# One attention-and-MLP kernel, five written-out instruction lists settled anew

## The chip, the cores and the metric

The kernel runs on one core of a Trainium2 chip. A core has five engines that matter here, each with its own in-order list of instructions: PE (TensorE, matrix products), DVE (VectorE), ACT (ScalarE), POOL (GpSimd) and SP (SyncE, which here only starts transfers). They meet through semaphores. The metric is the device time of one execution in microseconds, the median of a few runs. Before the change it is 328.6 us, the median of three runs between 327.31 and 330.21.

## What is computed

The input x has 2048 rows of 512 numbers. Four blocks follow one another, linear attention (A) and an MLP (B), each twice with the same weights, each with a residual sum and a layer norm in front:

```python
    x = x + _A_ref(_layernorm(x, axis=-1), A_wqkv, A_wo)
    x = x + _B_ref(_layernorm(x, axis=-1), B_w1, B_b1, B_w2, B_b2)
    x = x + _A_ref(_layernorm(x, axis=-1), A_wqkv, A_wo)
    x = x + _B_ref(_layernorm(x, axis=-1), B_w1, B_b1, B_w2, B_b2)
```

Attention has 32 heads of 16 numbers. With phi(t) = (t+1 if t > 0, else exp(t)) + 1e-6 it needs the sum over all rows of phi(k) times v (`kv`) and of phi(k) (`z`), and then gives each row phi(q)·kv / (phi(q)·z), times `wo`. So no output row of an attention block can start before all rows have passed through k. The MLP normalises its input again, multiplies by `w1` (512 to 1792), applies a tanh gelu with bias, multiplies by `w2` (1792 to 512) and adds `b2`; its rows do not depend on each other.

## The kernel before, in words

The 2048 rows are 16 row tiles of 128 (numbered st, 0 to 15) in 4 chunks of 512. Every piece of work is an operation with a name, built by `Graph.op`: `K1_9` is the k product of layer 1, row tile 9. The names that are used below, with the lines that issue them:

| names | what they do, engine | line |
|---|---|---|
| statsX, aggrX, vepsX, powX, nmrX, normX | layer norm of a row tile: DVE, DVE, POOL, POOL, POOL (only when ACT normalises), DVE or ACT | 734, 736, 739 or 747, 749, 766, 774 or 769 |
| TA, TB, TP | a transposing transfer, started by SP (PTA, PTB with tcA, tcB: the same by PE and a copy) | 784, 1069 (797, 807) |
| K, Q and expk, relu, min, phi | k and q products (PE), then phi on ACT, ACT, DVE, and DVE or POOL | 852, 870 or 883; 822, 833, 826 or 835, 828 or 839 |
| G, Z, KV, M | the products that make z and kv·wo (PE), with evictions ga, gt, kvm, cpm on DVE or ACT | 953 or 985, 934, 1008, 1031 |
| D or pz, red, den, rec, pr | the denominators, by PE and ACT or by DVE and POOL | 1077 to 1085, 1053 to 1065 |
| WO, then RA | attention output (PE) and residual sum (DVE) | 1101, 1106 |
| W1, gelu | MLP up (PE), gelu (ACT) | 1133, 1139 |
| W2 (two halves, _0 and _7), RB, OD | MLP down (PE), residual sum (DVE), output transfer (SP) | 1171, 1177 or 1181, 1183 |

`W10_1_3_0` is thus `W1`, layer 0, chunk 1, column tile 3 (of 14), part 0. Chunk 0 of each layer is cut into two halves of 256 rows (parts 0 and 1); all other `W1` operations take 512 rows.

The order of the work is written out by hand as data: `CONF["ORDER"]` holds one list of names per engine, 388 names for PE, 506 for DVE, 323 for ACT, 220 for POOL, 104 for SP. Each engine plays its list in that order and nothing is reordered on the chip. While the kernel is built, `Scheduler.run` walks the five lists with a model of durations (the numbers in the `G.op` calls). The model no longer decides any order. It decides which free slot of a buffer pool or which PSUM bank each tile takes (the one that the model says is free first), and so which earlier user an operation has to wait for. `assign_waits` then turns dependences and slot reuse into semaphore waits.

PSUM has 8 banks, shared by classes: `W1` results have banks 0 to 3, `W2` and `WO` results banks 3 to 5, two at a time. Two output buffers (`NOUT`), 12 large tiles (`t4`), 10 normalised tiles (`yb`) and 8 phi(k) tiles (`pkb`) are the pools that most tiles go through. ACT holds one function table at a time; a change between exp and gelu issues a table load (line 1304).

Of the kernel before, what the change touches and what calls it, by code (L numbers as in the profile page):

```python
# [7 lines left out]
ACT = mybir.ActivationFunctionType  # L8
# [102 lines left out]
class Scheduler:  # L111
# [12 lines left out]
    def run(self):  # L124
# [14 lines left out]
        for _ in g.ops:  # L139
# [29 lines left out]
            if o.fast and pool_busy > at:  # L169
                dur += pool_busy - at - 60.0  # L170
            if o.fast:
                dve_busy = at + dur
            if e == "pool" and o.sem is None and o.dur > 300.0:
                dur += max(0.0, min(dve_busy - at, 400.0))
                pool_busy = at + dur
# [92 lines left out]
def assign_waits(graph, order, sems, dma_sems):  # L268
# [10 lines left out]
    while len(done) < total:  # L279
        moved = False  # L280
        for e in ENGINES:
# [44 lines left out]
    LAND={'x0': 3210, 'x1': 3930, 'wk1': 5300, 'wk0': 6430, 'x2': 6950, 'wq': 8450, 'xc0': 9730, 'xc1': 11020, 'xc2': 12240},  # L326
# [1041 lines left out]
```

## Time and profile before

| quantity | value |
|---|---|
| median of three runs (lowest, highest) | 328.6 us (327.31, 330.21) |
| span of the profiled execution, first to last instruction | 326.2 us |
| the profiled execution's own device time | not listed apart from its span; the median is 2.4 us above it |
| PE matmul busy | 320.6 us, 98% |
| DVE, ACT, POOL busy | 218.7 us (67%), 197.5 us (61%), 131.2 us (40%) |
| bytes moved by DMA | 20.39 MB, mean 62 GB/s |
| chain that ended last, by engine | PE 91%, DVE 4%, DMA 2%, ACT 1% |

The profile lists, per engine and line of the kernel, how long instructions ran and what the engine waited for before them. Matmuls are pipelined: one of 512 columns is listed with 379 ns, while the next one starts 216 ns after it. The time between starts is what counts for PE.

### The profile page before, as it was taken

How to read it: one execution, taken by the hardware profiler on the slowest of the kernel's cores; microseconds unless marked ns; L12 is line 12 of the kernel's file. 1: busy time of each engine (PE TensorE's matmuls, PEld its weight loads, DVE VectorE, ACT ScalarE, POOL GpSimd, SP SyncE). 2: the span in 40 equal slices, each digit the busy share in tenths (PEclk: the TensorE clock that was granted, in tenths of full speed). 3: DMA queues.
4: the chain of work that ended last, by engine and by line, in shares of the span. 5: the costliest groups of instructions: out<-in, count | busy, mean ns of one | idle time of the engine just before them, and what ended most of it. 6: DMA issues, size and time to landing. Idle time of an engine off the chain costs nothing.

```text
span 326.2 us, 4796 instructions
## 1 busy us (share of the span) xinstructions
PE 320.6 (98%) x1724; PEld 158.2 (48%) x1724; DVE 218.7 (67%) x506; ACT 197.5 (61%) x338; POOL 131.2 (40%) x224
## 2 busy tenths in 40 slices
PE   7999999999999999999999999999999999999996
PEld 3444545656544444444444444458644444444453
DVE  4998689989866662535468899999988663300132
ACT  5998889744753387357963395969923553645200
POOL 3465637673238106134139525645811275100000
PEclk9999999999999999999999999999999999999999
DMA  7424662524012400312110200111153233300011
GB/s 239 163 51 92 173 223 62 181 49 81 21 31 48 97 1 2 74 22 55 27 32 19 47 17 0 28 39 36 32 92 72 48 45 69 81 0 2 32 64 50
DMA packets 47028, 20.39 MB, mean 62 GB/s; under 512 B 41948, under 2 KB 45532, under 8 KB 47004
## 3 DMA queue, kind: packets, MB, share of 16 engines
q1 hardware_dynamic: 45676, 15.09, 20.4%
q0 software_dynamic: 1056, 4.72, 4.5%
q10 hardware_dynamic: 272, 0.26, 0.3%
q8 instruction: 14, 0.23, 0.3%
q14 instruction: 10, 0.08, 0.1%
HBM read 8.00 MB, written 2.10 MB: 31 GB/s over the span
## 4 chain that ended last, share of the span: by engine, by line
PE 91%; DVE 4%; DMA 2%; ACT 1%; SPq 1%; issue 1%; ACTq 0%
PE ps L1133 29%; PE ps L1171 26%; PE ps L1101 9%; PE ps L852 9%; PE ps L870 5%; PE ps L953 4%; PE ps L883 3%; PE ps L985 2%; DMA t<-in_A_x_dram 1%; PE ps L1158 1%; DMA t<-yb 1%; DVE t L839 1%; PE ps L1008 1%; PE ps L1077 1%; PE ps L797 1%
## 5 line engine op out<-in xcount | busy, mean ns | idle before, releaser
L1139 ACT ACTIVATE gT<-ps,b1c 128x512 bf16<-128x512 f32 (+1 forms) x140 | 76.9, 601 | 61.2 <-PE ps L1133 60.8
L1133 PE MATMUL ps<-t,w 128*128 128x512 bf16 (+1 forms) x560 | 102.2, 336 | 0.5 <-DMA t<-yb 0.3
L1171 PE MATMUL ps<-w,gT 128*128 128x512 bf16 x434 | 97.3, 379 | 0.0
L1133 PEld LDWEIGHTS ps<-t,w 128*128 128x128 bf16 x560 | 54.4, 98 | 44.5 <-DMA t<-yb 0.7
L1171 PEld LDWEIGHTS ps<-w,gT 128*128 128x128 bf16 x434 | 42.4, 98 | 50.4 <-ACT gT L1139 0.3
L822 ACT ACTIVATE eb<-ps 128x512 bf16<-128x512 f32 x56 | 32.1, 606 | 21.3 <-PE ps L852 20.3
L749 POOL TENSOR_TENSOR rstd<-veps,neghalf 128x1 f32<-128x1 f32 x64 | 36.7, 581 | 8.2 <-DVE veps L747 5.5
L1181 DVE TENSOR_TENSOR outb<-ps,xsb 128x512 bf16<-128x512 f32 x15 | 10.3, 689 | 40.3 <-PE ps L1171 32.1
L734 DVE BATCH_NORM_STATS2 stats<-xsb 128x6 f32<-128x512 f32 x48 | 32.0, 681 | 0.2
L1101 PE MATMUL ps<-gtb,t 128*128 128x512 bf16 x128 | 31.8, 379 | 0.1
L852 PE MATMUL ps<-wqkv,t 128*128 128x512 bf16 x128 | 31.1, 379 | 0.0
L769 ACT ACTIVATE yb<-xsb,nmr,rstd 128x512 bf16<-128x512 f32 x21 | 16.8, 811 | 12.6 <-POOL nmr L766 12.5
L833 ACT ACTIVATE rb<-ps 128x512 bf16<-128x512 f32 x38 | 22.3, 611 | 1.6 <-PE ps L852 0.9
L739 POOL TENSOR_SCALAR veps<-mv 128x1 f32<-128x1 f32 x32 | 7.3, 227 | 38.4 <-DVE mv L736 36.6
L774 DVE TENSOR_SCALAR yb<-xsb,mv,rstd 128x512 bf16<-128x512 f32 x27 | 15.0, 572 | 9.0 <-POOL rstd L749 8.9
L835 DVE TENSOR_SCALAR eb<-eb 128x512 bf16<-128x512 bf16 x46 | 13.6, 306 | 10.9 <-ACT eb L822 10.8
L1118 POOL TENSOR_TENSOR xsb<-xsb,b2b 128x512 f32<-128x512 f32 x14 | 17.0, 1218 | 8.1 <-DVE yb L774 6.5
L870 PE MATMUL ps<-wqkv,t 128*128 128x512 bf16 x80 | 20.2, 379 | 0.0
L747 POOL TENSOR_SCALAR veps<-mv 128x1 f32<-128x1 f32 x28 | 8.4, 305 | 28.0 <-DVE mv L736 26.9
L1101 PEld LDWEIGHTS ps<-gtb,t 128*128 128x128 bf16 x128 | 12.3, 98 | 14.9 <-ACT gtb L966 0.7
L852 PEld LDWEIGHTS ps<-wqkv,t 128*128 128x128 bf16 x128 | 12.0, 97 | 14.7 <-ACT t L807 0.9
L1065 POOL TENSOR_TENSOR t<-t,rr 128x512 bf16<-128x512 bf16 x7 | 7.7, 1100 | 24.4 <-DVE rr L1061 14.1
(103 smaller groups left out, 398.7 us busy)
## 6 DMA issues: line engine op xcount, KB each, us to landing
w<-in_B_w_dram POOLq DMA_DIRECT2D x4, 896.0 KB, 5.9
out_dram<-outb SPq DMA_DIRECT2D x15, 128.0 KB, 2.1
t<-in_A_x_dram SPq DMA_DIRECT2D x3, 512.0 KB, 7.3
t<-yb SPq DMA_TRANSPOSE x56, 2.5
wqkv<-in_A_wqkv_dram SPq DMA_DIRECT2D x1, 512.0 KB, 5.7
wo<-in_A_wo_dram POOLq DMA_DIRECT2D x1, 512.0 KB, 6.6
wqkv<-in_A_wqkv_dram POOLq DMA_DIRECT2D x1, 512.0 KB, 4.5
t<-t SPq DMA_TRANSPOSE x20, 2.5
```

The lines of the kernel that those rows point to most:

```text
L734: G.op("dve", lambda e: e.bn_stats(stats[:, s.slot, :], src()), 620, reads=src_keys, writes=[k + "s"], tiles=[s, *src_tiles], prio=prio, n ...
L749: G.op("pool", lambda e: e.tensor_tensor(rstd[:, s.slot:s.slot + 1], veps[:, s.slot:s.slot + 1], neghalf[:], op=ALU.pow), 570, reads=[k + ...
L769: G.op("act", lambda e: e.activation(yb[:, y.slot, :], src(), ACT.Identity, bias=nmr[:, s.slot:s.slot + 1], scale=rstd[:, s.slot:s.slot + 1]),
L822: G.op("act", lambda e: e.activation(eb[:, et.slot, :], bank(bt), ACT.Exp, scale=factor()), 478, reads=[src_key, *more], writes=[f"e{tag}" ...
L833: G.op("act", lambda e: e.activation(rb[:, rt.slot, :], bank(bt), ACT.Relu, scale=factor()), 478, reads=[src_key, *more], writes=[f"r{tag} ...
L852: ins = e.matmul(bank(b), lhsT=yTa(yT)[:, dt, k * P:(k + 1) * P], rhs=wqkv[:, dt, D:2 * D], start=(dt == 0), stop=(dt == DT - 1))
L870: ins = e.matmul(bank(b), lhsT=yTa(yT)[:, dt, k * P:(k + 1) * P], rhs=wqkv[:, dt, 0:D], start=(dt == 0), stop=(dt == DT - 1))
L1101: ins = e.matmul(bank(wb), lhsT=yTa(pq)[:, kt, k * P:(k + 1) * P], rhs=gtb[:, kt, :], start=(kt == 0), stop=(kt == DT - 1))
L1118: G.op("pool" if on_pool else "dve", lambda e: e.tensor_tensor(xsb[:, st, :], xsb[:, st, :], b2b[:], op=ALU.add), 1120 if on_pool else 600 ...
L1133: ins = e.matmul(bank(b, n), lhsT=w1[:, dt, ft * P:(ft + 1) * P], rhs=yTa(yT)[:, dt, k0 * P:k1 * P], start=(dt == 0), stop=(dt == DT - 1))
L1139: G.op("act", lambda e, ft=ft, b=b, k0=k0, k1=k1, n=n: e.activation(gT[:, g.slot, ft * 512 + k0 * P:ft * 512 + k1 * P], bank(b, n), ACT.Ge ...
L1171: ins = e.matmul(bank(b), lhsT=gT[:, g.slot, ft * 512 + k * P:ft * 512 + (k + 1) * P], rhs=w2[:, ft, :], start=(ft == 0), stop=(ft == FT - 1))
```

## The change

No name is added or dropped in any of the five lists, no operation moves to another engine (the table `WAY` is the same), and no instruction's code changes. Three things change.

First, the model's rule for POOL and DVE holding each other up. Second, durations and latencies of the model, among them the landing times of the first transfers. Third, the five lists, each in a new order. The model's hunk and the shape of the others:

```diff
-            if o.fast and pool_busy > at:
-                dur += pool_busy - at - 60.0
             if o.fast:
+                dur += max(0.0, pool_busy - at - 130.0)
                 dve_busy = at + dur
-            if e == "pool" and o.sem is None and o.dur > 300.0:
-                dur += max(0.0, min(dve_busy - at, 400.0))
-                pool_busy = at + dur
+            if e == "pool" and o.sem is None:
+                dur += max(0.0, dve_busy - at - 130.0)
+                if o.dur > 700.0:
+                    pool_busy = at + dur
...
-    LAND={'x0': 3210, 'x1': 3930, 'wk1': 5300, 'wk0': 6430, 'x2': 6950, 'wq': 8450, 'xc0': 9730, 'xc1': 11020, 'xc2': 12240},
+    LAND={'x0': 3230, 'x1': 4500, 'wk1': 5300, 'wk0': 6320, 'x2': 7010, 'wq': 8490, 'xc0': 9780, 'xc1': 11060, 'xc2': 12290},
...
-                G.op("dve", lambda e: e.bn_stats(stats[:, s.slot, :], src()), 620, reads=src_keys, writes=[k + "s"],
-                     tiles=[s, *src_tiles], prio=prio, name=f"stats{tag}")
...
+                G.op("dve", lambda e: e.bn_stats(stats[:, s.slot, :], src()), 602, reads=src_keys, writes=[k + "s"],
+                     tiles=[s, *src_tiles], prio=prio, name=f"stats{tag}", lat=50)
...
-                 570, reads=[k + "v", "neghalf"], writes=[k + "r"], tiles=[s], prio=prio, name=f"pow{tag}")
+                 535, reads=[k + "v", "neghalf"], writes=[k + "r"], tiles=[s], prio=prio, name=f"pow{tag}", lat=45)
```

PE's list, the start, the middle of the first MLP, and the step from `K` of layer 1 to its attention output:

```diff
-            "warm PTA0_12 idle0_0 PTA0_13 idle0_1 K0_12 K0_13 PTA0_14 Q0_3_0 Q0_3_2 PTA0_15 K0_14 K0_15 G0_12_0 "
-            "Q0_3_1 G0_13_0 Q0_3_3 G0_14_0 PTA0_1 K0_0 G0_15_0 K0_1 Z0_3 G0_0_0 K0_3 K0_2 Q0_0_2 G0_1_0 Q0_0_0 "
...
-            "W20_0_7 W10_0_8_1 W10_0_1_1 W10_0_7_1 W10_0_9_1 W10_0_5_1 W10_0_12_1 W10_0_0_1 W10_0_3_1 W10_0_11_1 "
-            "W10_0_13_1 W10_1_3_0 W10_1_4_0 W10_1_13_0 W10_1_11_0 WO0_8_0 W10_1_0_0 WO0_9_0 W10_1_2_0 W10_0_6_1 "
...
-            "ZH1 Q1_0_3 Z1_3 G1_2_2 G1_3_1 D1_0_0 ZR1 G1_2_0 D1_0_2 G1_3_2 D1_0_1 G1_3_3 G1_3_0 G1_2_3 Q1_3_0 "
-            "KV1_0 KV1_1 Q1_3_1 KV1_2 D1_0_3 Q1_3_2 KV1_3 Q1_2_0 M1_1 M1_0 M1_3 M1_2 Q1_2_1 WO1_0_0 Q1_3_3 WO1_0_1 "
-            "WO1_1_0 WO1_0_2 WO1_0_3 WO1_3_0 WO1_2_0 Q1_2_2 WO1_5_0 WO1_4_0 PTB1_1 Q1_2_3 PTB1_0 WO1_6_0 "
...
+            "warm PTA0_12 idle0_0 PTA0_13 idle0_1 K0_12 K0_13 PTA0_14 Q0_3_0 Q0_3_1 PTA0_15 G0_12_0 K0_14 Q0_3_3 "
+            "K0_15 Q0_3_2 G0_13_0 K0_0 G0_14_0 Z0_3 G0_15_0 PTA0_1 K0_3 K0_1 Q0_0_0 K0_2 G0_0_0 Q0_0_2 Q0_0_3 G0_1_0 "
...
+            "W10_0_5_1 W20_1_7 W10_0_0_1 W10_0_7_1 W10_0_11_1 W10_0_3_1 W10_0_9_1 W10_0_4_1 W10_0_6_1 WO0_8_0 "
+            "W10_0_13_1 W10_0_2_1 W10_0_8_1 W10_0_12_1 WO0_11_0 W20_3_0 W10_1_3_0 W10_1_9_0 WO0_15_0 W10_1_4_0 "
...
+            "G1_2_3 G1_2_0 D1_0_1 G1_3_0 G1_3_2 D1_0_2 G1_3_3 KV1_0 KV1_1 Q1_3_1 D1_0_3 KV1_2 Q1_3_0 KV1_3 Q1_3_2 "
+            "Q1_2_0 M1_2 M1_3 M1_0 M1_1 Q1_2_1 WO1_0_0 WO1_0_1 WO1_0_2 WO1_0_3 WO1_1_0 Q1_3_3 WO1_2_0 Q1_2_2 WO1_5_0 "
```

SP's list around the same places, and where the last chunks of the second MLP are transposed:

```diff
-            "Tb1 TB0_1 TB0_2 TB0_3 TB0_5 TB0_6 TB0_7 TB0_4 TP0_2_1 TP0_2_0 TP0_2_3 TP0_3_3 TP0_2_2 TA1_0 TA1_1 "
...
-            "OD1 TP1_2_1 TB1_12 TB1_14 OD2 TB1_13 TB1_15 OD4 TB1_11 TB1_9 OD5 TB1_8 TB1_10 OD7 OD14 OD6 OD9 OD12 "
...
+            "TB0_1 b2 TB0_2 TB0_3 TP0_2_0 TP0_2_3 TB0_6 TB0_4 TB0_5 TB0_7 TP0_3_3 TP0_3_0 TP0_2_2 TP0_2_1 TP0_3_2 "
...
+            "TB1_14 TB1_12 TB1_13 OD2 TB1_15 TB1_9 OD6 TB1_11 TB1_10 TB1_8 OD7 OD13 OD5 OD4 OD8 OD12 OD10 OD9 OD15_0 "
```

DVE's list is reordered in the same way throughout. Between `RA0_0` and the last norm of chunk 1, for instance, it now also holds `pr0_2_0` and `pr0_2_3`, which came behind all of chunk 1's norms before. In POOL's list the first half of `w2` (`w2_0`) and the second (`w2_1`) change places as transfers, and `bdm1` moves to the front.

More of the change, by code (lines that the diff above doesn't have):

```diff
@@ L733, in norm @@
             else:
[L734 to L737 removed]
+                G.op("dve", lambda e: e.bn_stats(stats[:, s.slot, :], src()), 602, reads=src_keys, writes=[k + "s"],
+                     tiles=[s, *src_tiles], prio=prio, name=f"stats{tag}", lat=50)
+                G.op("dve", lambda e: e.bn_aggr(mv[:, s.slot, :], stats[:, s.slot, :]), 92, reads=[k + "s"], writes=[k + "m"],
+                     tiles=[s], prio=prio, name=f"aggr{tag}", lat=55)
                 if double:
                     G.op("pool", lambda e: e.tensor_scalar(veps[:, s.slot:s.slot + 1], mv[:, s.slot, 1:2], 1.0 + EPS, EPS * EPS,
[L740 removed]
+                                                           op0=ALU.mult, op1=ALU.add), 200, reads=[k + "m"], writes=[k + "v"],
                          tiles=[s], prio=prio, name=f"veps{tag}", lat=40)
@@ L821, in factor @@
                 return rstd[:, by[0].slot:by[0].slot + 1] if by else 1.0
-            G.op("act", lambda e: e.activation(eb[:, et.slot, :], bank(bt), ACT.Exp, scale=factor()), 478, reads=[src_key, *more], writes=[f"e{tag}"],
+            G.op("act", lambda e: e.activation(eb[:, et.slot, :], bank(bt), ACT.Exp, scale=factor()), 569 if by else 483, reads=[src_key, *more], writes=[f"e{tag}"],
                  tiles=[bt, et, *held], prio=prio, name=f"exp{tag}", lat=90, table="exp")
@@ L832, in phi @@
             rt = Tile(RB, f"r{tag}")
-            G.op("act", lambda e: e.activation(rb[:, rt.slot, :], bank(bt), ACT.Relu, scale=factor()), 478, reads=[src_key, *more], writes=[f"r{tag}"],
+            G.op("act", lambda e: e.activation(rb[:, rt.slot, :], bank(bt), ACT.Relu, scale=factor()), 569 if by else 478, reads=[src_key, *more], writes=[f"r{tag}"],
                  tiles=[bt, rt, *held], prio=prio, name=f"relu{tag}", lat=90)
             G.op("dve", lambda e: e.tensor_scalar(eb[:, et.slot, :], eb[:, et.slot, :], 1.0, 1e-6, op0=ALU.min, op1=ALU.add),
-                 210, reads=[f"e{tag}"], writes=[f"e{tag}"], tiles=[et], prio=prio, name=f"min{tag}", lat=80, fast=True)
+                 202, reads=[f"e{tag}"], writes=[f"e{tag}"], tiles=[et], prio=prio, name=f"min{tag}", lat=50, fast=True)
             on_pool = eng(f"phi{tag}") == "pool"
@@ L1058, in attn_den @@
                          reads=[f"l{tag}"], writes=[f"rd{tag}"], tiles=[r, d], prio=p, name=f"red{tag}", lat=60)
-                    G.op("dve", lambda e, d=d: e.tensor_scalar(rd[:, d.slot, :], rd[:, d.slot, :], 1e-6, None, op0=ALU.add), 100,
-                         reads=[f"rd{tag}"], writes=[f"rd{tag}"], tiles=[d], prio=p, name=f"den{tag}", lat=60)
-                    G.op("dve", lambda e, d=d: e.reciprocal(rr[:, d.slot, :], rd[:, d.slot, :]), 300,
+                    G.op("dve", lambda e, d=d: e.tensor_scalar(rd[:, d.slot, :], rd[:, d.slot, :], 1e-6, None, op0=ALU.add), 90,
+                         reads=[f"rd{tag}"], writes=[f"rd{tag}"], tiles=[d], prio=p, name=f"den{tag}", lat=60, fast=True)
+                    G.op("dve", lambda e, d=d: e.reciprocal(rr[:, d.slot, :], rd[:, d.slot, :]), 262,
                          reads=[f"rd{tag}"], writes=[f"rr{tag}"], tiles=[d], prio=p, name=f"rec{tag}", lat=60)
@@ L1140, in mlp_up @@
                         gT[:, g.slot, ft * 512 + k0 * P:ft * 512 + k1 * P], bank(b, n), ACT.Gelu_apprx_tanh, bias=b1c[:, ft:ft + 1], scale=1.0),
-                        144 + 0.833 * n, reads=[f"h{L}_{c}_{ft}_{hf}", "b1c"], writes=[f"g{L}_{c}_{ft}_{k}" for k in range(k0, k1)],
+                        156 + 0.833 * n, reads=[f"h{L}_{c}_{ft}_{hf}", "b1c"], writes=[f"g{L}_{c}_{ft}_{k}" for k in range(k0, k1)],
                         tiles=[b, g], prio=p, name=f"gelu{L}_{c}_{ft}_{hf}", lat=110, table="gelu")
```

9 lines of the change are left out of this document (3 added, 6 removed), and 257 rows, old and new, of the table ORDER.

## The prediction

> **What bounds the kernel now.** I read the busy table first, then the clock row, then the groups by shape, the waits of PE, and the chain of work that ended last.
>
> ```profile
> span 326.2 us, 4796 instructions
> ...
> PE 320.6 (98%) x1724; PEld 158.2 (48%) x1724; DVE 218.7 (67%) x506; ACT 197.5 (61%) x338; POOL 131.2 (40%) x224
> ...
> PEclk9999999999999999999999999999999999999999
> ...
> PE 91%; DVE 4%; DMA 2%; ACT 1%; SPq 1%; issue 1%; ACTq 0%
> ```
>
> PE is busy 98% of the span, at full clock, and 91% of the last chain is PE. Busy alone could hide slow matmuls, so I count starts. In the timeline a 512-column matmul starts 216 ns after the one before, a 256-column one 109, a 128-column one 55 and a 1-column one 25. From the groups by shape, leaving out warm-up and idle fillers: 1304 of 512 columns are 281.7 us, 252 of 256 are 27.5, 64 of 128 are 3.5, 88 of one column are 2.2, together **314.9 us**. PE starts its first real work at 4.57 us, waits until 6.14 for the second row tile, and ends at 323.7. From 6.14 on, the starts leave only **2.5 us** over the count. Behind PE's end lie 2.5 us of sum and output transfer.
>
> A rule of the Trainium skill speaks against this reading: "Perfetto Trace Analysis", section "Identifying the Most-Contended Engine", calls matmul busy time a poor measure and wants weight-load busy time and the share of peak arithmetic instead. The first is 48% here and would leave half the span to win; the second, 24.3 GFLOP in 326.2 us against the page's 78.6 TFLOP/s, is an estimated 95%. The starts 216 ns apart decide for the second; by the first, far more than 2.5 us could go, and I give it no chance of its own.
>
> **Where the 2.5 us are.** In the timeline of PE:
>
> ```profile
> 202.03 1.03 PE L870 MATMUL ps<-wqkv,t 128*128 128x512 bf16 x4
> 203.32 0.62 PE L1008 MATMUL ps<-gtb,wqkv 128*128 128x128 bf16 x8 [0.27 <-DVE gtb L998]
> ```
> ```profile
> 267.77 4.05 PE L1171 MATMUL ps<-w,gT 128*128 128x512 bf16 x18
> 272.07 2.12 PE L1133 MATMUL ps<-t,w 128*128 128x512 bf16 x9 [0.26 <-DMA t<-yb]
> ```
>
> Four matmuls from 202.03 free PE at 202.89, `KV1_0` starts at 203.32: 0.43 us lost. Eighteen from 267.77 free it at 271.66: 0.41 lost. Counted like that, the losses are 0.69 in the start (five places, 8.4 to 36.4), 0.41 at 78.8, 0.43, 0.19 and 0.10 at 203.3, 206.1 and 210.3, 0.28 at 247.0 and 0.41 at 272.1. The one at 78.8 (`W10_1_3_0`) is a transfer of which 15 parts land by 77.2 and the last at 78.72; no list can foresee that. So the change can win 2.5 us at most, and can lose without limit: with PE full, every new wait of PE lengthens the run by as much.
>
> **The change, part by part.** I lay the new PE list end to end at these starts, from `K0_12` at 6.55 us as before, and call the result "by the count". Where another engine's list matters I add its rows up at their start-to-start times (DVE: 0.60 us for a 512-wide f32 or PSUM operation, 0.46 a norm, 0.34 a phi, 0.26 `rec`, 0.20 `min`, 0.09 `aggr` and `den`).
>
> *The model's numbers* issue nothing. They choose slots and banks, and so waits. No row shows a wait of that kind on PE; I take 0, between 0 and 1 us.
>
> *Table loads.* Going through ACT's list, exp and gelu change 13 times before and 13 times after, 1283 ns each, never on PE's path. 0.
>
> *Weights.* In POOL's and SP's lists transfers change places: `w2_0` comes last, behind `pr0_1_1` at about 53, and takes the 5.9 us of its row; `W2` wants it at 66.8. `b2` stands behind `TB0_1` (59.3), takes 3.0, and is wanted at about 67. 0, since 4 us and more cover both.
>
> *The start.* `G0_12` goes ahead of `K0_14`, which takes away the 0.06 and 0.19 us that `K0_14` and `K0_15` waited for ACT's copies. `Z0_3` comes 2.4 us earlier, at 17.4 by the count. DVE's list up to `phik0_15`, from `phik0_12` at about 9.7 and with its waits, ends near 17.6, and `normA0_1` behind it near 19.0, while `PTA0_1` wants it at 18.6. `Q0_0_0`, at 20.6, waits for `TA0_2`, whose norm ends near 18.5 and whose transfer takes 2.5. Each is about 0.4 late, and PE pays the 0.4 once. I take +0.4 and −0.25.
>
> *First MLP, 60 to 130 us.* `WO0_8`, `WO0_11`, `WO0_15` and `WO0_12` come 5, 11, 19 and 15 us earlier (77.6, 80.2, 84.3, 101.8 by the count), `W10_1_3_0` 4 later (82.6). So DVE must do `pr0_2_0` and `pr0_2_3` ahead of chunk 1's last norms. From `RA0_0` (53.9) the list adds up to 17.6 us until `pr0_2_0`, 18.5 until `pr0_2_3`; with 2.5 us of transfer `WO0_8` has its data at 74.0 and `WO0_11` at 74.9. `normB0_5`, the last norm, ends at 76.7, of which 0.8 is a wait for `W20_1_7`. SP starts transposes 1.25 us apart, so `TB0_7`, fourth behind `TP0_2_3`, starts at 78.8 and lands at 81.3; `W10_1_3_0` wants it at 82.6. It holds by 1.3 us if DVE runs at its sum. Before, the same kind of stretch, `RA0_0` to `pr0_2_2`, added up to 29.6 us and took 34.0, 15% more; some of that was DVE waiting for POOL's `pow`, and the new list puts the norms further behind it. Its 22.0 us with 15% more put `TB0_7` at 83.8, 1.2 late. I take +0.3, between 0 and 1.2. The 0.41 at 78.8 goes, since the same lateness would now be covered.
>
> *Layer step, 190 to 218 us.* Between `G1_3_3` and `KV1_0` there was a `Q1` product, now there is none, and `KV1_0` comes 0.9 us earlier by the count. What DVE does from `phik1_14` to `gt1_0` falls from 7.8 to 6.7 us, because `phiq1_1_3` and `gt1_2` now come later; `gt1_3` stands 9.6 behind `phik1_14`, before 10.6. So the 0.43 and 0.19 go. All of `WO1_0` now follows `M1` with one `Q1` between (before, two ahead of all but its first part): three `cpm` copies on ACT (line 966, 0.6 us each, with their signals about 2.0) must fit into the 2.1 us between `M1_2` and `WO1_0_3`, so up to 0.3 late. The 0.10 goes, +0.2 comes.
>
> *Second MLP.* The chain of work shows how `W11_3_2_0` came late:
>
> ```profile
> 266.26 0.45 SPq L784
> ...
> 266.75 1.51 SPq L1183
> ...
> 268.31 1.19 SPq L784
> ...
> 269.54 2.49 DMA t<-yb
> ```
>
> An output transfer (`OD2`, 1.5 us) stood ahead of two transposes. In the new list one transpose (`TB1_15`) stands behind `OD2`, and all four wait for `RA1_8` at most, whose product ends at 254.4 by the count. Adding POOL's and ACT's rows from there, the last of the four lands near 266, and `W11_3_5_0` wants it at 268.0: the 0.41 goes with 2 us to spare, although PE wants it 4 us earlier than before. `WO1_12` wants `TP1_3_0` at 244.5 and I find it landed near 241: the 0.28 goes. The tail keeps its last product, sum and transfer: 0.
>
> Sum: −0.25 −0.41 −0.72 −0.28 −0.41 = −2.1, and +0.4 +0.3 +0.2 plus 0.2 for places not seen = +1.1. Net **−1.0 us** on the profiled span, 325.2. The profiled execution's own time is not listed; the median of 328.6 stands 2.4 us above its span. I take the same 2.4 for after: **327.6 us**. The three runs before differ by 2.9 us, so about 1% (3.3 us) is what a measurement here can tell from no change.
>
> **Rivals.**
>
> *Everything fits (10%).* All 2.5 us go and nothing comes: 326.1. For it: my margins are mostly above 1 us. Against: the start leaves under 0.2 us in several places.
>
> *The losses only move (22%).* As many new waits as old ones, up to 1.5 us more: 328 to 330, about 329. For it: the old list left 11 such places, and a transfer's late part can fall anywhere.
>
> *DVE falls behind from 60 to 110 us (16%), the slower side.* Mechanism: POOL and DVE lengthen each other. In the rows of line 1059 the same small operation takes from 111 to 1130 ns:
>
> ```profile
> L1059 DVE TENSOR_SCALAR rd<-rd x20: 111/181/1130, 54.0 to 248.8; 128x32 f32<-128x32 f32 x20
> ```
>
> If other pairs now meet, `TB0_7` is late, and `WO0_15` and `WO0_10` behind it. It costs nothing until DVE is 1.3 us late at `normB0_5`, at 15% it costs 1.2, and at 30% (22.0 us become 28.6, 5.8 behind the 76.7) 4.5 at that place in place of the 0.3: 331.8, where over 1% slower begins. Against: the old stretch was 15%, and PE had no loss there. The Trainium skill's "GPSIMD Engine Reference", section "Key points", says that GpSimd shares its memory interfaces with VectorE and contends with its two-input and two-port operations. By that rule a new order makes new collisions; the trace agrees with the 1130 ns.
>
> *The lists do not do what they say (2%).* The names are the same 1541, so this would be slot choice alone: a bank held late behind ACT, some 0.7 us each time (a gelu's 0.60 us and the signal), 328 to 329.
>
> **How the numbers follow.** The forecast, 326.5 to 328.3, has 50%. Faster by over 1% (under 325.3) needs all of the 2.5 us and a lucky median too: 6%. Slower by over 1% (over 331.9) is the worse part of the third rival and waits that I did not see: 15%. The rest, 79%, is within 1%. The range must leave out no more than 20%: from 325.4, just past the floor, to 331.6.
>
> **What would show it.** Right: PE starts without gaps at 203, 206, 247 and 272 us, `W10_1_3_0` on time near 83, at most 1.5 us over the count from 6.14 on, 13 table loads. Wrong: a PE wait for a transpose (line 784) between 80 and 92, DVE more than 1.3 us behind at `normB0_5`, or waits of PE for line 966 behind the `M1` products of more than 0.3 us.

## The result, and where the time went

The changed kernel is slower by a third of a per cent: 329.17 us against 328.19 us in the median of 20 runs each, a ratio of **1.0033 (95% interval 1.0019 to 1.0047)**. Forecast were 327.6 us and a ratio below one. In four later sets of runs the kernel before had medians of 328.2 to 328.7 us.

The page of the changed kernel, its first lines, its clock row and the shares of the chain that ended last:

```profile
span 326.7 us, 4795 instructions
...
PE 321.2 (98%) x1724; PEld 158.5 (49%) x1724; DVE 218.2 (67%) x506; ACT 197.8 (61%) x338; POOL 134.3 (41%) x224
...
PEclk9999999999999999999999999999999999999999
...
PE 87%; DMA 4%; DVE 3%; POOL 2%; ACT 2%; issue 1%; SPq 1%; ACTq 0%
```

PE is as busy as before and at the same clock, but its share of the chain has fallen from 91% to 87%: DMA, DVE, POOL and ACT now have links in it. POOL is busy 3.1 us longer with the same 224 instructions.

The same count of starts as in the prediction (216, 109, 55 and 25 ns) gives the losses of PE over the count from 6.2 us on. "Start" is up to 60 us, "middle" up to 190, "end" the rest:

| loss of PE, us | before | after | the larger ones after |
|---|---|---|---|
| start | 0.83 | 2.35 | `PTA0_14` 0.26, `Q0_3_0` 0.19, `Z0_3` 0.47, `G0_15_0` 0.24, `PTA0_1` 0.28, `Q0_0_0` 0.21, `K0_7` 0.55 |
| middle | 0.38 | 0.67 | `PTB0_0` 0.21, `K1_0` 0.29, `W10_2_3_0` 0.20 |
| end | 1.44 | 0.67 | `PTB1_1` 0.54, `W11_2_2_0` 0.12 |
| sum | 2.65 | 3.69 | |

The difference, 1.04 us of 326, is 0.32%. That this is so close to the ratio is in part chance: the two profiled spans, 326.2 and 326.7 us, differ by only half of it, because in the profile after the second row tile landed 0.63 us sooner and PE began that much earlier. All the places from 78.8 us on that were to be mended are mended: at 78.8, 203, 206, 210, 247 and 272 us PE no longer waits. So the gains came, and more than their sum was lost at places that did not wait before. This is PE's timeline at two of them, the start and 217 us:

```profile
17.71 0.55 PE L930 MATMUL ps<-onesm,pkb 128*128 128x1 bf16 x16 [0.30 <-DVE pkb L835]
18.37 1.04 PE L949 MATMUL ps<-pkb,yb 128*128 128x512 bf16 x4
19.52 0.38 PE L793 MATMUL ps<-idp,yb 128*128 128x128 bf16 x4
```
```profile
213.83 2.75 PE L1097 MATMUL ps<-gtb,t 128*128 128x512 bf16 x12
216.95 0.40 PE L793 MATMUL ps<-idp,yb 128*128 128x128 bf16 x4 [0.37 <-ACT yb L765]
```

(The number of a line in the new file is 4 less than that of the same line in the old one.) In the first, four products from 18.37 free PE at 19.24 and `PTA0_1` starts at 19.52, 0.28 late. In the second, twelve from 213.83 free it at 216.42, and `PTB1_1` starts 0.53 later.

**Who is late.** Both places hang on a normalisation by ACT, and it on one small operation of POOL. The timelines of ACT at the start, of POOL at 214 us and of DVE beside it:

```profile
12.91 1.26 ACT L829 ACTIVATE rb<-ps,rstd 128x512 bf16<-128x512 f32 x2
15.16 0.81 ACT L765 ACTIVATE yb<-t,nmr,rstd 128x512 bf16<-128x512 bf16 x1 [0.99 <-POOL nmr L762]
15.88 0.67 ACT L818 ACTIVATE eb<-ps,rstd 128x512 bf16<-128x512 f32 x1
...
17.59 0.72 ACT L752 ACTIVATE yb<-yb,rstd 128x512 bf16<-128x512 bf16 x1
...
18.68 0.69 ACT L829 ACTIVATE rb<-ps,rstd 128x512 bf16<-128x512 f32 x1
```
```profile
214.16 0.72 POOL L745 TENSOR_TENSOR rstd<-veps,neghalf 128x1 f32<-128x1 f32 x1
214.98 1.07 POOL L762 TENSOR_SCALAR nmr<-mv,rstd 128x1 f32<-128x1 f32 x1
```
```profile
214.99 0.68 DVE L1061 TENSOR_TENSOR t<-t,rr 128x512 bf16<-128x512 bf16 x1
215.58 0.42 DVE L835 TENSOR_TENSOR t<-eb,rb 128x512 bf16<-128x512 bf16 x1
```

At 15.16 ACT's `normA0_3` has waited 0.99 us for POOL, and behind it on ACT stands `expk0_15`, which the k tile 15 and with it `Z0_3` need. What follows on ACT is late too. `yscA0_15` (17.59) ends at 18.31, and `G0_15_0` starts 0.06 later. `reluq0_3_2` (18.68) ends at 19.38 and so frees the PSUM bank that `PTA0_1` was given; `PTA0_1` starts 0.14 later, though the norm that it transposes, `normA0_1`, had ended at 18.89. Its 0.28 us are therefore a wait for a bank.

At 214.98 `nmrB1_1`, 128 numbers, takes 1.07 us (0.27 before), while DVE does `pr1_1_3` and `phiq1_3_0`. Over both traces I fitted the lengthening of POOL's 306 small operations of the norms to what DVE ran beside them: each microsecond beside a DVE sum or product of two SBUF operands (`pr`, `pz`, `za`, the bias add) lengthens POOL's operation by 0.6 to 0.8 us, beside `min`, `phi` and `norm` by 0.3 to 0.6, beside `stats`, `red` and everything that reads PSUM by nothing (below 0.1). The Trainium skill's "GPSIMD Engine Reference", section "1. Specifications", names just that pairing, VectorE instructions with two SBUF inputs or in a two-port mode; the trace agrees, with the 1.07 us. What those operations cost is a matter of who meets whom, and the new order made other pairs.

### The profile page after: what moved, and what is told of

Same layout as the page of the kernel before. It is cut to its first block, busy times and chain, and to the rows that moved or that the text cites. A ratio compares the mean times of both kernels' runs of the same rounds, so it can differ in the third digit from the quotient of the medians.

```text
span 326.7 us, 4795 instructions
## 1 busy us (share of the span) xinstructions
PE 321.2 (98%) x1724; PEld 158.5 (49%) x1724; DVE 218.2 (67%) x506; ACT 197.8 (61%) x338; POOL 134.3 (41%) x224
## 4 chain that ended last, share of the span: by engine, by line
PE 87%; DMA 4%; DVE 3%; POOL 2%; ACT 2%; issue 1%; SPq 1%; ACTq 0%
PE ps L1129 30%; PE ps L1167 28%; PE ps L848 6%; PE ps L1097 6%; PE ps L981 4%; PE ps L866 3%; PE ps L879 3%; PE ps L949 3%; DMA t<-in_A_x_dram 2%; DMA t<-yb 2%; DVE stats L730 1%; PE ps L1154 1%; ACT yb L765 1%; PE ps L1073 1%; DVE xsb L1102 1%
## 5 line engine op out<-in xcount | busy, mean ns | idle before, releaser
L1129 PE MATMUL ps<-t,w 128*128 128x512 bf16 (+1 forms) x560 | 103.9, 336 | 0.0
L1167 PE MATMUL ps<-w,gT 128*128 128x512 bf16 x434 | 99.7, 379 | 0.0
L745 POOL TENSOR_TENSOR rstd<-veps,neghalf 128x1 f32<-128x1 f32 x64 | 38.5, 612 | 4.3 <-DVE veps L743 1.9
L770 DVE TENSOR_SCALAR yb<-xsb,mv,rstd 128x512 bf16<-128x512 f32 x27 | 15.2, 570 | 10.0 <-POOL rstd L745 9.7
```

The costliest lines, as they stand in the source:

```text
L745: G.op("pool", lambda e: e.tensor_tensor(rstd[:, s.slot:s.slot + 1], veps[:, s.slot:s.slot + 1], neghalf[:], op=ALU.pow), 535, reads=[k + ...
L1129: ins = e.matmul(bank(b, n), lhsT=w1[:, dt, ft * P:(ft + 1) * P], rhs=yTa(yT)[:, dt, k0 * P:k1 * P], start=(dt == 0), stop=(dt == DT - 1))
L1167: ins = e.matmul(bank(b), lhsT=gT[:, g.slot, ft * 512 + k * P:ft * 512 + (k + 1) * P], rhs=w2[:, ft, :], start=(ft == 0), stop=(ft == FT - 1))
```

## The experiments

A kernel's time is given as its ratio to the kernel before on the same chip, with the 95% interval.

### Half of the lists at a time

All five lists have a place between 52 and 60 us at which both orders have done the same operations. So the old start can stand ahead of the new rest, and the new start ahead of the old rest (with the old model numbers, because the old rest under the new numbers comes to a point at which no operation finds a free slot; so there is no run of the new numbers under the old lists, and their share stays open).

```diff
 # old_start: after.py; ORDER up to ZR/KV of layer 0 as in before.py, in all five lists
-  "... Q0_3_0 Q0_3_1 PTA0_15 G0_12_0 K0_14 Q0_3_3 K0_15 ..."
+  "... Q0_3_0 Q0_3_2 PTA0_15 K0_14 K0_15 G0_12_0 Q0_3_1 ..."
 # new_start: before.py with the opposite exchange
```

> The changed kernel with the old order of its first 52 to 60 us in all five lists; the model's numbers and the rest of the lists are the new ones. Beyond the count of starts, and without transfers whose last part straggles, the two profiles lose 0.69 us (before) and 1.7 us (after) in the start, 0 and 0.7 between 60 and 190 us, 1.4 and 0.7 behind 190 us. Theory 1 (the new start costs 1.0 us, the rest gives and takes 0.7): the loss is gone, 1.000 of the time before (0.999 to 1.001), no waits at 17.7 to 21.7 us. Theory 2 (the loss is not in the start but in slots chosen by the new model numbers, or in the middle): 1.002 to 1.0035, as after.

> The kernel before, with its old model numbers, and the new order of the first 52 to 60 us alone. Theory 1 (the new start costs 1.0 us by itself): 1.003 of the time before, with the waits at Z0_3, PTA0_1 and Q0_0_0 between 17 and 22 us, 0.7 to 1.2 us together. Theory 2 (slots by the new model numbers, or the middle): 1.000, and no waits there beyond 0.3 us.

Measured: `old_start` **1.0023 (1.0007 to 1.0038)**, `new_start` **1.0147 (1.0126 to 1.0168)**. The number of `old_start` is that of theory 2; the number of `new_start` is neither's. In the trace of `old_start` the waits at 17 to 22 us are gone, but `W10_1_3_0`, on time in the trace after, is 0.68 late at 84.8, and the middle loses 1.71 us in place of 0.67. `new_start` has waits at `Z0_3`, `G0_15_0` and `PTA0_1` (0.36, 0.24 and 0.28), none at `Q0_0_0`, where one was expected, and something that the cut itself made: the new start has `b2` late in SP's list, the old rest wants it early. The waits of its DVE between 58 and 72 us:

```profile
DVE xsb L1114 <- DMA b2b<-in_B_b_dram: 3.4, 1, 3.4
```

So its 1.5% says little of the start. What the pair left was the question why a place behind the cut, with the same order in both, is on time in one run and 0.7 us late in another.

### Two single places

```diff
 # norm3_back: after.py, ACT's list
-  "... reluk0_14 normA0_3 expk0_15 reluk0_15 expq0_3_2 ..."
+  "... reluk0_14 expk0_15 reluk0_15 normA0_3 expq0_3_2 ..."
 # dve217: after.py, DVE's list
-  "statsB1_0 aggrB1_1 RA1_2 aggrB1_0 minq1_3_0 statsB1_2 pr1_1_3 phiq1_3_0 aggrB1_2 RA1_3 normB1_0 "
+  "statsB1_0 aggrB1_1 pr1_1_3 RA1_2 aggrB1_0 minq1_3_0 statsB1_2 aggrB1_2 RA1_3 phiq1_3_0 normB1_0 "
```

> The changed kernel, with normA0_3 moved in ACT's list from ahead of expk0_15 to behind reluk0_15. Theory 1a (ACT stands still from 14.1 to 15.2 us because normA0_3 waits for POOL's nmrA0_3, and the k tile 15 behind it is late for Z0_3): phik0_15 starts about 0.7 to 1.0 us earlier, the waits at Z0_3, G0_15_0 and PTA0_1 (1.0 us together) go, and 0.5 to 1.0 us come back: 1.0005 to 1.002 of the time before. Theory 1b (DVE's own list, not ACT, makes phik0_15 and normA0_1 late): phik0_15 stays within 0.3 us of 17.2 and nothing comes back, 1.003.

> The changed kernel, with two operations of DVE's list moved out of the time in which POOL does nmrB1_1: pr1_1_3 goes ahead of RA1_2, phiq1_3_0 behind RA1_3. In the profile after, nmrB1_1 took 1.07 us beside those two (0.27 before) and PTB1_1 lost 0.54 us behind it. Theory 1 (POOL's small operation is held up by DVE's pr and phi): nmrB1_1 takes 0.26 to 0.4 us, PTB1_1 loses under 0.15, and the time falls by 0.4 to 0.5 us, to 1.002 of the time before. Theory 2 (PTB1_1 is late because the chain from RA1_1 is late, however long POOL takes): nmrB1_1 short or not, PTB1_1 still loses 0.4 or more.

Measured: `norm3_back` **1.0035 (1.0019 to 1.005)**, `dve217` **1.0055 (1.004 to 1.007)**: no gain, and a loss, where both were to bring something back. The mechanisms are right in both. In `norm3_back` `phik0_15` starts at 16.31 (17.23) and the waits at `Z0_3`, `G0_15_0` and `PTA0_1` are gone; but `normA0_3` now ends 0.34 later, its transfer `TA0_3` is issued 0.35 later and lands 3.2 us after its issue (2.4 in the kernel after; an 8 KB packet of kind "instruction", of which more below, runs beside it at 17.57), and `K0_3` is 0.71 late. In `dve217` POOL's operation is short:

```profile
216.70 0.55 POOL L745 TENSOR_TENSOR rstd<-veps,neghalf 128x1 f32<-128x1 f32 x1
217.35 0.26 POOL L762 TENSOR_SCALAR nmr<-mv,rstd 128x1 f32<-128x1 f32 x1
```

0.26 us where it was 1.07, and PE does not wait at `PTB1_1`. But `phiq1_3_0` is later, ACT's `reluq1_3_3` waits 0.73 for it (the slot), `tcB1_1` and `tcB1_0` stand behind that on ACT, and `WO1_6_0` is 0.88 late for its bank. A wait that is filled by taking time from a neighbour came back here at the neighbour. The rest of its loss is not at 217 us at all: `Q0_0_0` lost 1.43 us (0.21 after), because one of 16 parts of its transfer `TA0_2` landed at 22.71, 1.77 after the other 15. And `W10_1_3_0` was late again, 0.54 and 0.78 us in these two.

### What makes a part of a transfer late

The trace lists every packet of the DMA engines. Among them are 16 KB packets of kind "instruction", 13 or 14 in a run, one for about every 125 products of PE. In `dve217` one of them runs from 20.54 to 21.63, beside `TA0_2`; in the kernel before one runs from 76.62 to 77.67, beside the transfer whose last part, at 78.72, I had called a straggler. In the 17 traces of this case 35 parts land more than 1 us after their fellows (behind the first 10 us), and beside 34 of them such a fetch is under way or ended in the 3 us before, though fetches with that margin cover about a sixth of the time. SP's transposes, 1.19 to 1.27 us each to issue, take more than 1.6 us 42 times of 1309; 38 of the 42 overlap a fetch, of all only 89 do. So a fetch slows a transpose beside it in two ways, its issue and its last part.

There are smaller fetches too, 8 KB, ten in a run. With them counted, all 35 late parts and all 42 long issues lie beside a fetch. The other way round, of the transposes issued from 10 us on in the 17 traces, 1035 have no fetch of either size under way between the start of their issue and 1.25 us after its end, and every one of them lands 1.18 to 1.30 us after that end. Of the 257 others 83 land more than 1.5 us after it.

Two losses of the new start are of this kind. In the trace after, a 16 KB fetch at 18.69 stretches the issue of `TA0_2` to 1.83 us, and `Q0_0_0` loses 0.21 behind it. And an 8 KB fetch at 33.22 lies beside `TA0_7`, the last of these three transposes:

```profile
L780 SPq DMA_TRANSPOSE t<-yb x3: 1188/1264/1264, 30.2 to 32.7; - x3
...
DMA to landing us min/median/max: 2.4/2.5/3.2
```

It is issued at 31.40 and lands at 34.58. PE is free for `K0_7` at 34.17; with the 2.5 us of the others `TA0_7` would have been there at 33.9, so the 0.55 at `K0_7` is this transfer's. In all seven kernels with the new start such a fetch lies beside `TA0_7`, and `K0_7` is late. In the ten with the old start none does, and `K0_7` loses nothing. No run moves this fetch away: with a longer stream of PE it comes at 33.50 (`after_shift`) and 32.41 (`after_shift39`), still beside `TA0_7`.

To test the 16 KB fetches, PE's instruction stream is made longer ahead of the work, in the idle time before the first row tile, so that all fetches of PE's stream come earlier:

```diff
 # before_shift and after_shift
-    N_WARM2=1,
+    N_WARM2=33,
-    N_WARM=8,
+    N_WARM=0,
 # warm-up: 33 products of 128 columns for 8 of 512 and one of 128
```

> The kernel before, with its warm-up products cut smaller: 33 of 128 columns in place of 8 of 512 and one of 128, the same columns in the same idle time, so that PE's instruction stream is 24 products longer ahead of the real work. Theory A (a transfer's last part is late when one of PE's 16 KB instruction fetches goes through the same DMA engine; the fetches come every 128 products, so they now come 24 of 128 of a distance earlier, 4 to 6 us): the fetch at 76.6 us comes at 71 to 73, the last part of the transfer that W10_1_3_0 waits for is no longer late at 78.7, its 0.41 us go, 0.998 to 0.9995 of the time before. Late parts appear beside the new places of the fetches. Theory B (late parts are chance, or belong to the transfer): the late part stays at 78.7 or falls where no fetch is, 1.000.

> The changed kernel with the same longer warm-up stream. Theory A (instruction fetches slow the transposes beside them, their issue on SP too): the fetch at 77 us comes at 72, where SP issues no transpose; SP's issue of TB0_6 takes 1.2 to 1.3 us (2.03 in the profile after, beside the fetch), W10_1_3_0 is on time, the late parts at 243.5 and 270.8 us go or lie elsewhere. 1.001 to 1.003 of the time before; nothing is won in the start. Theory B (chance): late parts at places without a fetch, W10_1_3_0 late by 0.5 to 0.8 us as in three of the other kernels, 1.003 to 1.004.

Measured: `before_shift` **0.9967 (0.9957 to 0.9977)**, `after_shift` **1.0004 (0.9993 to 1.0014)**. The direction of theory A in both, and more of it than it promised: each number lies below the ranges of both theories. The queue view of the kernel before from 76 to 78.8 us, packets, MB, share, and the median from issue to landing, and the same of `before_shift`:

```profile
q1 hardware_dynamic: 1065, 0.26, 65.7%
q8 instruction: 1, 0.02, 2.3%
...
t<-yb SPq DMA_TRANSPOSE x1, 4.0
```
```profile
q1 hardware_dynamic: 1236, 0.30, 52.7%
...
t<-yb SPq DMA_TRANSPOSE x1, 2.5
```

With the fetch at 72.3 in place of 76.6 there is no instruction packet in that stretch, the transpose lands 2.5 us after its issue in place of 4.0, and `W10_1_3_0` starts on time (the whole middle loses 0.01 us). The spans of the runs draw together as well: 325.2 to 326.2 us, where the kernel before had 325.8 to 328.1 beside it; after_shift 326.1 to 327.1, but for one at 328.0, and the changed kernel 325.9 to 329.2. So 0.41 us in one profile can be 1.1 us in the median: the profiled run of the kernel before, 326.2, was among its better ones, and what a fetch meets must differ from run to run (argued from the spans; only one run in each set has a trace). The late part is not chance, as I had it; its place follows the instruction stream.

The changed kernel gained as much from the same edit, 0.29%. So PE's 16 KB fetches explain the spread, but not the difference between the two kernels: with them moved it is 1.0004 to 0.9967, **0.37%** (0.23 to 0.52 by the two intervals), as large as without.

### Filling the places

```diff
 # mended: old_start, and in PE's list
-  "... WO0_6_0 PTB0_0 WO0_5_0 ...", "... K1_0 W20_6_0 W10_2_3_0 K1_1 ..."
+  "... WO0_6_0 WO0_5_0 PTB0_0 ...", "... W20_6_0 K1_0 K1_1 W10_2_3_0 ..."
-  "... WO1_4_0 PTB1_1 Q1_2_3 PTB1_0 WO1_6_0 WO1_7_0 ..."
+  "... WO1_4_0 Q1_2_3 PTB1_1 WO1_6_0 PTB1_0 WO1_7_0 ..."
 # and in DVE's
-  "... rec0_3_3 red0_3_0 RB0_1 normB0_7 normB0_4 normB0_5 ..."
+  "... rec0_3_3 normB0_7 normB0_4 RB0_1 normB0_5 red0_3_0 ..."
 # mended_shift: the same with the longer warm-up
```

> The old order of the first 52 to 60 us and the new one behind it, with the places where the changed kernel lost time given other work: PTB0_0 behind WO0_5_0, W20_6_0 and K1_1 ahead of W10_2_3_0 with K1_0 between them, PTB1_1 behind Q1_2_3 and PTB1_0 behind WO1_6_0 in PE's list, RB0_1 and red0_3_0 behind the norms of chunk 1 in DVE's. Theory 1 (each of these losses is a place of its own and can be filled): 0.85 us in the start, 0.2 to 0.7 in the middle, 0.15 behind 190 us, against 2.65 in the kernel before: 0.995 to 0.998. Theory 2 (a wait that is filled comes back at the next operation, as two mends of single places have shown): 1.000 to 1.002.

> The kernel of old start, new rest and filled places, with the longer warm-up stream too. Theory A: SP's issue of TP0_2_3 takes 1.2 us (2.8 beside a fetch at 75.6 us in the kernel with the old start alone), W10_1_3_0 on time, 0.2 to 0.5 us less than without the shift: 0.994 to 0.997. Theory B: the same as without the shift, within 0.1%.

Measured: **1.0121 (1.0103 to 1.0138)** and **1.0053 (1.0039 to 1.0066)**. `mended` goes the way of theory 2, and worse than it said, but not at all the places alike; the time of `mended_shift` is in the range of neither theory, and of its forecast only SP's issue came. The first two moves of PE's list work: nothing is lost at `PTB0_0` or at `K1_0`. The move at 217 us costs most: PE comes to the `W1` products of layer 1 only 0.35 us after `tcB1_0` on ACT has ended, ACT has yet to load its table (220.11 to 221.39), the `W1` results have four banks, and the fourth product already waits for a gelu; one gap of 0.67 and six of 0.29 follow. Another 0.94 stands at `W10_1_2_0`, in both runs with the move in DVE's list: with it the building of the kernel gives `W10_1_2_0` the PSUM bank of `W10_1_6_0`, the product just ahead of it (in `old_start` that of `W10_1_4_0`), and PE waits for the gelu that empties this bank. So the choice of banks has a price here. The shift alone is worth 0.68% here; in `mended` SP's issue of `TP0_2_3` takes 2.77 us beside a fetch, in `mended_shift` 1.19.

### The lists without the fetches

```diff
 # old_start_shift: old_start with 33 products of 128 columns in the warm-up
 # fill2_shift: the same, and of the moves above only PTB0_0 and K1_0/W20_6_0/K1_1
```

> The kernel of old start and new rest, with the longer warm-up stream (33 products of 128 columns). With PE's instruction fetches away from SP's transposes at 76 us, only the lists are left to compare: the changed kernel with this stream took 1.0004 of the time before, and its start loses about 1.2 us more than the old one. Theory 1 (the new start costs 1.0 to 1.3 us, the rest of the new lists is as good as the old): 0.996 to 0.9975, as the kernel before with this stream (0.9967). Theory 2 (the start costs nothing, the new lists lose in the middle and at the end): 1.000.

> The same with two places filled in PE's list: PTB0_0 behind WO0_5_0, and W20_6_0 ahead of K1_0 with K1_1 ahead of W10_2_3_0. In the last profile with these two, PE lost nothing at either place. Theory 1 (both losses, 0.21 and 0.49 us in the profile after, can be filled): 0.5 to 0.7 us less than without, 0.994 to 0.996. Theory 2 (they come back elsewhere): the same as without, within 0.1%.

Measured: `old_start_shift` **0.9985 (0.9977 to 0.9993)**, `fill2_shift` **0.9966 (0.9953 to 0.9978)**. Against `after_shift` (1.0004) the old start is worth 0.19%, 0.6 us, half of theory 1. Against `before_shift` (0.9967) the new rest costs another 0.6 us, and filling the two places in the middle brings just that back. Each 0.19% is a difference of two medians and known to some 0.4 us; and `after_shift` and `before_shift` ran on another chip than these two, each against the kernel before on its own chip. The first difference of this kind, `old_start`, had hidden it: there a fetch at 75.6 lay beside `TP0_2_3`. Its queue view from 75.4 to 78.3 us, and that of `old_start_shift`:

```profile
q8 instruction: 1, 0.02, 4.8%
q14 instruction: 1, 0.01, 1.6%
...
t<-t SPq DMA_TRANSPOSE x1, 3.9
```
```profile
q14 instruction: 1, 0.01, 0.7%
...
t<-t SPq DMA_TRANSPOSE x1, 2.4
```

From the issue of `TP0_2_0` to the end of that of `TP0_2_3` SP took 4.39 us in the first and 2.75 in the second, `TB0_7` stood behind them on SP, and `W10_1_3_0` was late or on time.

### The dose

```diff
 # before_shift12: before.py with N_WARM=4, N_WARM2=17
 # before_shift39: before.py
-        idle("warm", [D] * cf["N_WARM"] + [P] * cf["N_WARM2"])
+        idle("warm", [88] * 48)
```

> The kernel before, with 12 products more in the warm-up in place of 24 (four of 512 columns and 17 of 128). Theory A (place of the fetches): the fetch at 76.6 us comes at 74 to 75, beside SP's issue of TB0_7 or TB0_4, which takes 0.7 to 1.6 us longer, so that W10_1_3_0 is on time or late by up to 1; the time lies between those of no shift and of 24 products, 0.997 to 1.000, and differs more from run to run than with 24. Rival (the finer warm-up itself makes the kernel faster): half of the gain of 24 products, 0.998 to 0.9985, and spans as close together as with 24.

> The kernel before, with 39 products more in the warm-up (48 of 88 columns, the same columns). Theory A: the fetch at 76.6 us comes at 68 to 71, beside TB0_2 to TB0_5; W10_1_3_0 has 6 us until then and is on time, but other fetches meet other transfers (near 196, 218, 235, 260 us), so no more is gained than with 24 products: 0.996 to 0.9985. Rival (the finer warm-up itself makes it faster): 0.995.

Measured: 12 products more **1.0012 (0.9996 to 1.0027)**, 24 more 0.9967, 39 more **0.9962 (0.9949 to 0.9975)**. Twelve should have been half of the gain if the finer warm-up itself made the kernel faster; it is none, and 1.0012 lies above the ranges of both. The place was not where I had it: the fetch of 76.6 came at 73.2 and cost PE nothing, but another, at 221.6, met the transpose `TB1_3`. The view of line 784 (the transposes) from 216 to 226 us in `before_shift12`, and in the kernel before from 219:

```profile
L784 SPq DMA_TRANSPOSE t<-yb x2: 1188/1189/1190, 218.7 to 220.3; - x2
...
DMA to landing us min/median/max: 2.4/3.4/4.4
```
```profile
L784 SPq DMA_TRANSPOSE t<-yb x2: 1188/1188/1189, 219.5 to 221.1; - x2
...
DMA to landing us min/median/max: 2.4/2.4/2.4
```

Of the two transposes one lands 4.4 us after its issue in place of 2.4, and PE's timeline shows who paid:

```profile
224.75 2.45 PE L1133 MATMUL ps<-t,w 128*128 128x256 bf16 x21 [1.22 <-ACT gT L1139]
```

PE stood 1.22 us (the view names ACT, but ACT was itself idle for want of PE; the transfer landed at 224.65). These 1.22 us alone would hide more than half of the gain of 24 products, so the time of `before_shift12` does not by itself speak against the finer warm-up. The traces do: outside the places where a fetch made a transfer late, PE loses some 2.0 to 2.2 us over the count in the kernel before, in `before_shift` and in `before_shift12` alike, so the finer warm-up wins PE nothing there. With 39 more, the spans of the five runs lie within 0.5 us (325.0 to 325.5).

### What is left

```diff
 # after_shift39, fill2_shift39: 48 products of 88 columns; norm3_mid_shift: after_shift, and in ACT's list
-  "... reluk0_14 normA0_3 expk0_15 reluk0_15 expq0_3_2 ..."
+  "... reluk0_14 expk0_15 normA0_3 reluk0_15 expq0_3_2 ..."
```

> The changed kernel with 39 products more in the warm-up (48 of 88 columns). Theory 1 (the lists cost about 1.2 us more than the old ones, 0.37%, wherever the fetches fall, and the rest of the spread is their place): 0.999 to 1.0005 of the time before, against 0.9962 for the kernel before with this warm-up. Theory 2 (all of the slowdown is the place of the fetches): 0.996 to 0.997.

> The changed kernel with 24 products more in the warm-up, and normA0_3 moved in ACT's list behind expk0_15 alone. Theory 1 (ACT standing still at normA0_3 makes Z0_3, G0_15_0 and PTA0_1 late): expk0_15 starts near 14.5 us, the k tile 15 is done 0.7 to 1.0 us earlier, TA0_3 is not later than before the move, and 0.5 to 1.0 us come back: 0.9975 to 0.999, against 1.0004 without the move. Theory 2 (DVE's list makes them late, or the next transfer does): 1.000 to 1.001.

> Old start, new rest, the two filled places and 39 products more in the warm-up. If the gains add up: 0.994 to 0.9965 (0.9966 with 24 products more, and 39 gave the kernel before 0.0005 more than 24). If a fetch meets a transfer that PE waits for at its new place: 0.998 to 1.000, with a transfer that lands 1 to 2 us late beside it.

Measured: `after_shift39` **1.0000 (0.9974 to 1.0026)**, `norm3_mid_shift` **0.9979 (0.9959 to 0.9998)**, `fill2_shift39` **0.9961 (0.994 to 0.9981)**; the first two by theory 1. A second placement of the fetches leaves 0.38% between the lists (0.09 to 0.67 by the two intervals). And one name moved by one place in ACT's list brings back 0.25%, 0.8 us (0.03 to 0.47%). ACT in `norm3_mid_shift`:

```profile
14.26 0.76 ACT L818 ACTIVATE eb<-ps,rstd 128x512 bf16<-128x512 f32 x1
15.20 0.81 ACT L765 ACTIVATE yb<-t,nmr,rstd 128x512 bf16<-128x512 bf16 x1 [0.18 <-POOL nmr L762]
15.92 0.67 ACT L829 ACTIVATE rb<-ps,rstd 128x512 bf16<-128x512 f32 x1
```

`expk0_15` fills the time in which POOL is held up, `normA0_3` starts at the same 15.2 as in the kernel after, and of the waits named for the start only `PTA0_1` (0.28) and `K0_7` (0.68) remain. Here only idle time is used; in `norm3_back`, with `reluk0_15` ahead as well, 0.3 us were taken from `normA0_3` too, and a slow transfer came on top, so that the two runs do not measure the second step by itself. `fill2_shift39` gained nothing over 24 products. The two fastest kernels, `before_shift39` and `fill2_shift39`, both beat before and after, by 0.4% against the kernel before; their intervals do not tell them apart.

## Why the prediction was wrong

With PE's 16 KB fetches moved, the new lists cost **0.37% of 328 us, 1.2 us**, by either warm-up. Half of that is the start: 0.6 us by `old_start_shift` against `after_shift`, 0.8 by `norm3_mid_shift`; the 0.3 to 0.8 us of `K0_7`, beside an 8 KB fetch that no run moved, are part of what the start costs. The other half is the rest of the lists (`old_start_shift` against `before_shift`), and filling two places of the middle brings as much back. The profiles put the end 0.7 us in favour of the new lists, which these medians do not show; a difference of two of them is certain to 0.4 to 0.5 us, and to 0.7 to 1 us where `after_shift39` or `norm3_mid_shift` stands in it, so whether that gain reaches the median stays open. Step by step:

- **What can be won.** Right. PE loses 2.65 us in all, counted as forecast; every place named for a gain gave it.
- **A late part "no list can foresee".** Wrong. It lands late beside an instruction fetch of PE, whose place follows from the length of the stream. Moved, it is gone, and the kernel before is 0.33% faster with no change of its order, as much as the forecast hoped the new order would bring (1.0 us).
- **The model's numbers, 0.** PE has at least one wait for a bank in the trace after, `PTA0_1`'s 0.28. `new_start`, with the old numbers, has the same wait for the same bank, so it comes with the order. In `mended` a bank chosen otherwise cost 0.94, so the term could not be put at nothing in general. The new numbers alone were not tried.
- **Table loads and weights, 0.** Right: 13 loads, no wait of PE for a weight. `new_start` shows what the margin of `b2` is worth when it is gone: 3.4 us of DVE.
- **The start, +0.4.** This is the first step that failed, and not by its chain: `phik0_15` was to end at 17.6 and ended at 17.65, `normA0_1` at 19.0 and ended at 18.89. "PE pays the 0.4 once" is what was wrong. It paid four times, 1.20 us together, and each time for something else: at `Z0_3` 0.47 for `phik0_15`, as forecast; at `G0_15_0` 0.24 for ACT's `yscA0_15`; at `PTA0_1` 0.28 for a bank that ACT frees, not for `normA0_1`; at `Q0_0_0` 0.21 for a transfer whose issue a fetch stretched. One cause behind the first two is ACT standing still at `normA0_3`: in `norm3_mid_shift`, where `expk0_15` fills that time, `Z0_3` and `G0_15_0` no longer wait. That the second row tile landed 0.63 us sooner in this profile than in the one before is not the reason: in `dve217` `K0_12` starts at 6.45, near the 6.55 of the forecast, and the first three still lose 0.86. `K0_7` was in no term: its norm came at 30.5 in place of 25.9 and used up the margin, and the 8 KB fetch beside `TA0_7` made 0.55 of it, 0.27 to 0.76 in the other runs of the new start.
- **First MLP, +0.3.** Its own price held in the profile (0.0) and not in other kernels with the old warm-up: 0.54 to 0.78 in the three with the same order of the middle (`norm3_back`, `old_start`, `dve217`), 0.83 in `mended`. That it cost nothing in the profile after is the luck of where the fetch fell. The cause is not the one that I priced, DVE falling behind by 15%: from the start of `RA0_0` to the end of `normB0_5` DVE took 23.7 us against the 22.8 of the forecast, 4%. It is SP's issue, stretched by a fetch.
- **Layer step, −0.72 and +0.2; second MLP, −0.69.** The gains came. The wait behind the `M1` products did not; in its place stands `PTB1_1`, 0.54 late, which I had not looked at.
- **Places not seen, 0.2.** The second step that failed, and the larger one: `K0_7`, `PTB0_0`, `K1_0`, `W10_2_3_0`, `PTB1_1` and `W11_2_2_0` are 1.9 us in the profile after. With the 1.20 of the start the new losses are 3.1 us where the sum had 1.1; the gains of 2.1 came. Of about 390 operations of PE I had laid a dozen against their inputs.
- **Span to median, +2.4.** A constant in sign only: in these runs the time outside the span is 1.7 to 1.8 us (2.0 to 3.0 in some runs of the changed kernel; in the profiled one its last fetch comes at 329.0, behind the end of the work). The rest of the 2.4 was the profiled run's luck: the median span before is 326.5 to 326.9, not 326.2.

Of the rivals, "the losses only move", with 329 us, is the one that came. The mechanism of the third, POOL and DVE lengthening each other, has a part in two of the places; I had it at 60 to 110 us, and it showed at 15 and at 215. For the other places no run shows it: `Q0_0_0` and `K0_7` wait for a transfer beside a fetch, `K1_0`, `W10_2_3_0` and `W11_2_2_0` for transfers too, `PTB0_0` for its norm on DVE. What was to show it wrong (a wait for a transpose between 80 and 92) did show, in four other kernels and not in the profile after.

## What to carry to other kernels

When PE is full, a reordering is worth what it does to every operation's margin, not to the handful that wait: lay the whole new list against its inputs, and count each place with less than half a microsecond as a loss. Before lists are settled again, look at the packets of kind "instruction": if a transfer's last part or a transpose's issue is long beside one, some more or fewer instructions ahead of the work move all of that engine's, and that won more here than the order did. Give a waiting engine's idle time to what stands behind the wait, but no more than that idle time: one operation moved into it ahead of `normA0_3` brought 0.8 us, while the moves that took time from a neighbour (`dve217`, `mended`) cost 0.88 us at the next bank in the first and about 2.4 us in seven gaps in the second.

## What was not expected of the hardware

- Instruction fetches share the DMA engines with the kernel's transposes. A 16 KB packet takes 0.9 to 2.2 us, and a transpose beside it lands up to 2.7 us later (5.1 in place of 2.4, `TP0_2_0` in `old_start`) or takes up to 2.9 us to issue in place of 1.2 (`dve217`). The smaller fetches, 8 KB, did it too, with 0.65 us at `TA0_7` in the trace after, and beside `TA0_7` in all seven kernels with the new start.
- The finer warm-up has a price of its own at times. In the profiled run of `after_shift` the first products start 427 ns apart until 9.8 us, in place of 216, though the mean granted clock of that run reads 1.000. PE's timeline:

```profile
6.84 3.37 PE L848 MATMUL ps<-wqkv,t 128*128 128x512 bf16 x8
10.05 0.39 PE L793 MATMUL ps<-idp,yb 128*128 128x128 bf16 x4
```

  Eight products in 3.2 us, 1.5 more than at 216 ns; that run took 329.7 us, the others of this kernel 327.9 to 328.9. In `fill2_shift39` the first four products start 427 ns apart too. Three other runs with a finer warm-up (one each of `before_shift12`, `after_shift39` and `norm3_mid_shift`) show a granted clock of 0.995, all the rest 0.998 or more, and each is the longest of its kernel. The Trainium skill's "TensorE: Matmul & The Clock Gate", section "Part 1: The HAM clock gate (the "warmup" mystery)", gives 426.7 ns for a product of 512 columns on a cold array and ties warmth to a free-running window of activity; the 427 ns agree, and no run here shows the window.
- A fetch at the very end counts too: the time outside the span, 1.7 to 1.8 us in most runs, is 3.0 in the profiled run of the changed kernel, whose last fetch starts 2.3 us after the span's end. Its median over the 20 runs of the changed kernel is 1.9 us, so about 0.2 of the 1.0 us between the medians lies behind the span. That the fetch is the cause was not tested, and two runs speak against so simple a rule: in `old_start` and `dve217` the last fetch starts 1.2 and 1.1 us after the span's end, and the time outside is 1.85 and 1.76.
